# Attention and two expert layers on one core: token rows of the first block turned later, routing lists in two tables, probabilities stored as 18 rows, the second block's list loaded ahead of its weights

## The chip, the cores and the metric

The kernel runs on one core of a Trainium2 chip. The metric is device microseconds (us) of one execution. Before the change three runs gave 1200.1 (median), 1199.29 and 1203.38 us.

## What is computed

```python
def reference(**kwargs):
    attn_out = _attn_ref(**attn_kwargs)          # q halved by mean of pairs, softmax(q k^T / 8) v
    x = attn_out.transpose(0, 2, 1, 3).reshape(B, S, H * D)     # 4 x 576 tokens of 512
    x = _moe_ref(x=x, **moe_kwargs)              # r * ((relu(xk w_k))**2 w_v), r = sigmoid(xr w_r)
    return _moe2_ref(x=x, **moe2_kwargs)

def _moe2_ref(x, w_gate, w_local, w1, w2):       # 8 experts, one for each token
    logits = x @ w_gate
    local_gate = sigmoid(x @ w_local)
    # along a row of tokens: e = argmax(logits) where s == 0 or local_gate < 0.5, else the token before's e
    out[b, s] = softmax(logits)[e] * (relu(x[b, s] @ w1[e]) @ w2[e])
```

There are 32 heads of 1152 keys and 576 pooled queries, 2304 tokens, and eight experts of 512 x 1024 and 1024 x 512. Products of float32 are made as three matmuls of a high and a low part.

## The kernel before, in words

The program is one stream, written out by hand in a fixed order; every engine works its own part of it in that order. Names: PE is TensorE, ACT ScalarE, DVE VectorE, POOL GpSimd, and SP is the engine that issues most DMAs. An engine that waits holds up everything behind it on that engine.

**Attention** (to about 540 us) is not touched.

**The first layer** works on units `u` of 256 tokens (two tiles `i` of 128), 0 to 8. For a unit, `hidden` makes one of four groups of 256 hidden features (24 matmuls of 128x256), `square` squares them on ACT and makes the low part on POOL (L748), `gate` makes the sigmoid gate of a tile (12 matmuls), `value` the second product (24 matmuls), and `product` (L774) multiplies and stores the rows to `x2d` in DRAM. `logits` (L783) makes nine dot products on DVE for a tile, each over two operands in SBUF. `mix` and `mix_split` prepare the next units' inputs; the low part is made on POOL (L568). In the loop over `u` (2 to 7) the parts of neighbouring units are interleaved.

**Routing** runs behind it, a unit at a time: `route1` (DVE) makes `kg`, `route2` turns it into a row on PE (L832), ACT copies it (L836), a DVE scan carries the expert along the tokens (`erow`, L838), `route3` spreads it over the partitions (L849, `oh` at L850), and `route4` counts the places (L857 to L869) and scatters the token numbers into the table `tbl` in DRAM: two indirect DMAs on POOL, one for each tile (L871). Both write the same tile, so the second waits until the first has landed.

**The second layer** works on blocks of up to 512 tokens of one expert. `early` (in unit 7) picks the largest expert from units 0 to 6, loads the block's list of tokens (`load_ids(0)`, L1015), its first weights (`load_w`), and gathers its rows (`gather_x(0, 0)`, L1029). The last unit, 8, is written out after the loop; in it `transpose_x(0)` turns the gathered rows on PE (L1054) and `gather_x(0, 2)` fetches the other half, right after the first `gate`. Weights come as raw chunks (0.5 MB each, L988 and L994) that `split_w` cuts into a high part on ACT (L1010) and a low part on DVE (L1011). `up` is the first product of a block (L1068), `down` the second (L1085), `finish` scales the rows by their probability (`pgs`) on ACT and scatters them to the output (L1093, L1094). A block with at most 128 tokens in a pair of tiles runs `lone_up` and `lone_down` (L1120, L1140).

After block 0's first half, the list of all blocks is made (`block_list`, `block_list2`), SP reads it into registers (`block_regs`, L977 and L978), loads five chunks of block 1's weights, then the lists of blocks 1 and 2, and stores the probabilities: `probabilities` ends with one DMA from 128 partitions x 18 to the 2304 places of `pd` (L1217), 4 bytes each. `gather_x(1, 0)` and `gather_p` (L1037, the probabilities of block 0's tokens) follow on POOL. All engines read the block counts into registers (L1355, L1356). Then `NH0[0] = 2` chunks of block 1 are split before block 0's second half goes through `up`; then come `finish` of the first half, `next_x(0)` (the rows of block 1 are turned, those of block 2 gathered), the other splits, and the second half's `down`. From there `block(j)` repeats for j = 1 to 12, the later ones only as far as the list has blocks.

Of the kernel before, what the change touches and what calls it, by code (L numbers as in the profile page):

```python
# [37 lines left out]
def kernel(  # L38
# [39 lines left out]
    tbl = dram.tile([E * NTS, 1], I32, name="tbl")  # L78
# [41 lines left out]
    ids = [cp.tile([P, 4], I32, name=f"ids{i}") for i in range(4)]  # L120
    pgs = [cp.tile([P, 4], F32, name=f"pg{i}") for i in range(2)]
# [11 lines left out]
    def constants2(tp, ci, pi):  # L133
# [3 lines left out]
        nc.gpsimd.iota(tid, pattern=[[P, NT]], base=0, channel_multiplier=1)  # L137
# [21 lines left out]
    def constants3(tp):  # L159
# [5 lines left out]
        nc.sync.dma_start(tbl.rearrange("(p f) o -> p (f o)", p=P), pad)  # L165
# [688 lines left out]
    def route4(u):  # L854
# [15 lines left out]
        for i in range(2):  # L870
            nc.gpsimd.indirect_dma_start(  # L871
                out=tbl, out_offset=bass.IndirectOffsetOnAxis(ap=si[:, i : i + 1], axis=0),
                in_=tid[:, 2 * u + i : 2 * u + i + 1], in_offset=None,
            )
# [96 lines left out]
    NH0 = (2, 2, 0)  # L971
# [41 lines left out]
    def load_ids(j):  # L1013
        if j <= JX:
            nc.sync.dma_start(  # L1015
                ids[j % 4], tbl[bass.ds(regs[j][1], 512), :].rearrange("(i p) o -> p (i o)", p=P),
                allow_slow_non_contiguous=True,
            )


    def gather_x(j, t):
        if j > JX:
            return
        for i in range(2):
            ix = bass.IndirectOffsetOnAxis(ap=ids[j % 4][:, t + i : t + i + 1], axis=0)
            if j:
                nc.gpsimd.indirect_dma_start(out=XGB[j % 2][:, i], out_offset=None, in_=x2d, in_offset=ix)
            else:
                nc.gpsimd.indirect_dma_start(  # L1029
                    out=XGB[0][:, i], out_offset=None, in_=x2d[0 : 256 * (NU - 2)], in_offset=ix,  # L1030
                    bounds_check=256 * (NU - 2) - 1, oob_is_err=False,
                )
# [170 lines left out]
    def probabilities():  # L1203
# [13 lines left out]
        nc.sync.dma_start(  # L1217
            pd[0:NTOK].rearrange("(t p) o -> p (t o)", p=P), pe, allow_slow_non_contiguous=True
        )
# [70 lines left out]
    transpose_x(0)  # L1290
    gather_x(0, 2)
# [6 lines left out]
    product(u, 0, py[1])  # L1298
    split_w(1)
# [43 lines left out]
    for j in (1, 2):  # L1343
        block_regs(j, lst[:, 0, j - 1 : j], lst[:, 1, j - 1 : j])
    for s in range(8, 8 + NRAW):
        load_w(s)
    load_ids(1)
    load_ids(2)
    probabilities()
    gather_x(1, 0)  # L1350
    gather_p(0, 0)
    gather_p(0, 2)
    down(0, 2)
    down(0, 3)
# [106 lines left out]
```

## Time and profile before

| what | value |
|---|---|
| median of three runs | 1200.1 us |
| the profiled execution's own time, its span | 1199.74 us, 1198.0 us |
| PE busy | 1080.2 us, 90% |
| DVE, ACT, POOL busy | 828.2, 718.6, 575.3 us |
| DMA | 156.31 MB, 130 GB/s in the mean |
| POOL's wait at L871 for the scatter before it | 67.2 us in 9 waits |

The profile is one execution. Times in its rows are microseconds from the span's start; an engine's row in the timeline gives start, duration, engine, line, operation, tiles and shapes, and in square brackets the idle time before it with what ended it. A `q` behind an engine's name is its sequencer: register reads, branches and the issue of DMAs. PE is busy nearly all the time from the attention's end on, so the places where it stands idle are the ones to look for; there are few, and three groups of them lie where the change works: in the steps of the loop over `u` (640 to 830 us), in unit 8 (830 to 858 us) and around the start of the second block (888 to 916 us).

### The profile page before, as it was taken

How to read it: one execution, taken by the hardware profiler on the slowest of the kernel's cores; microseconds unless marked ns; L12 is line 12 of the kernel's file. 1: busy time of each engine (PE TensorE's matmuls, PEld its weight loads, DVE VectorE, ACT ScalarE, POOL GpSimd, SP SyncE). 2: the span in 40 equal slices, each digit the busy share in tenths (PEclk: the TensorE clock that was granted, in tenths of full speed). 3: DMA queues.
4: the chain of work that ended last, by engine and by line, in shares of the span. 5: the costliest groups of instructions: out<-in, count | busy, mean ns of one | idle time of the engine just before them, and what ended most of it. 6: DMA issues, size and time to landing. Idle time of an engine off the chain costs nothing. (4 is left out here: it accounts for less than half of the span.)

```text
span 1198.0 us, 18084 instructions
## 1 busy us (share of the span) xinstructions
PE 1080.2 (90%) x6073; PEld 910.6 (76%) x6073; DVE 828.2 (69%) x1255; ACT 718.6 (60%) x1006; POOL 575.3 (48%) x392
## 2 busy tenths in 40 slices
PE   7899999999999999978999989897987999998875
PEld 6677777777777777767887878776776888876764
DVE  6888888888888888889955665685353544446544
ACT  5787777777777777767775444341333535446543
POOL 2556666666666666468734333342213514144233
PEclk9999999999999999998999999998897999999988
DMA  9166666656566564515520322203646756556765
GB/s 198 32 132 148 138 142 141 140 130 131 131 149 141 137 138 100 157 45 172 182 98 10 36 31 32 36 18 89 117 81 153 253 178 202 176 179 213 251 205 176
DMA packets 147348, 156.31 MB, mean 130 GB/s; under 512 B 62993, under 2 KB 115857, under 8 KB 146324
## 3 DMA queue, kind: packets, MB, share of 16 engines
q1 hardware_dynamic: 140836, 141.51, 47.4%
q0 software_dynamic: 6384, 13.15, 3.7%
q8 instruction: 73, 1.20, 0.5%
q14 instruction: 55, 0.45, 0.1%
HBM read 107.30 MB, written 15.58 MB: 103 GB/s over the span
## 5 line engine op out<-in xcount | busy, mean ns | idle before, releaser
L403 PE MATMUL pvt<-sr,V 128*128 128x288 f32 x1152 | 328.5, 409 | 31.4 <-ACT xc L416 14.7
L403 PEld LDWEIGHTS pvt<-sr,V 128*128 128x128 f32 x1152 | 202.1, 190 | 71.2 <-POOL sr L389 17.9
L345 PE MATMUL pt<-kw 128*128 128x288 f32 x1152 | 247.3, 337 | 5.5 <-DVE Mt L357 4.1
L389 POOL TENSOR_TENSOR sr<-sr,Mb 128x576 f32<-128x576 f32 x96 | 142.5, 1487 | 195.3 <-ACT Mb L380 159.5
L357 DVE TENSOR_TENSOR Mt<-Mt,pt 128x576 f32<-128x576 f32 x224 | 168.1, 750 | 76.2 <-ACT sr L349 74.3
L349 ACT ACTIVATE sr<-pt 128x576 f32<-128x576 f32 x288 | 181.5, 646 | 54.6 <-PE pt L345 52.4
L345 PEld LDWEIGHTS pt<-kw 128*128 128x128 f32 x1152 | 177.6, 189 | 34.8 <-DVE Mt L357 10.4
L396 ACT ACTIVATE sr<-sr 128x1728 f32<-128x1728 f32 x96 | 157.9, 1644 | 52.0 <-DVE sr L390 46.4
L390 DVE TENSOR_TENSOR sr<-sr,Mb 128x1152 f32<-128x1152 f32 x96 | 160.9, 1676 | 2.8 <-ACT Mb L380 2.8
L727 PE MATMUL ph<-a,wk 128*128 128x256 f32 x864 | 108.4, 286 | 0.9 <-ACT kr L745 0.4
L727 PEld LDWEIGHTS ph<-a,wk 128*128 128x128 f32 x864 | 106.5, 193 | 2.6 <-ACT kr L745 1.0
L767 PE MATMUL py<-kw,sq 128*128 128x512 f32 x312 | 84.3, 423 | 0.0
L1068 PE MATMUL ph<-a,wk 128*128 128x256 f32 x576 | 73.4, 288 | 6.3 <-PEq L1415 5.8
L1085 PE MATMUL py<-kw,sq 128*128 128x512 f32 x324 | 78.3, 398 | 0.0
L1068 PEld LDWEIGHTS ph<-a,wk 128*128 128x128 f32 x576 | 71.3, 195 | 8.8 <-issue 7.7
L871 POOL DMA_INDIRECT tbl<-tid,si x18 | 18.4, 1021 | 122.9 <-DMA tbl<-tid,si 67.2
L745 ACT ACTIVATE kr<-ph 128x512 f32<-128x512 f32 x36 | 21.3, 592 | 92.4 <-PE ph L727 57.2
L446 POOL TENSOR_TENSOR xo<-xc,t 64x576 f32<-64x576 f32 x32 | 73.1, 2283 | 1.2
L783 DVE CUSTOM_DVE_ANT_0 a<-r,wg 128x512 f32<-128x512 f32 x96 | 71.4, 744 | 3.1
L767 PEld LDWEIGHTS py<-kw,sq 128*128 128x128 f32 x312 | 62.1, 203 | 15.0 <-issue 0.2
L1085 PEld LDWEIGHTS py<-kw,sq 128*128 128x128 f32 x324 | 60.8, 189 | 14.5
L1037 POOL DMA_INDIRECT pg<-pd,ids x44 | 44.4, 1009 | 37.4 <-DMA pg<-pd,ids 15.7
(250 smaller groups left out, 1756.7 us busy)
## 6 DMA issues: line engine op xcount, KB each, us to landing
wraw<-in_moe_w_dram SPq DMA_DIRECT2D x101, 512.0 KB
kw<-Hk SPq DMA_DIRECT2D x224, 72.0 KB
ql<-in_q_dram SPq DMA_DIRECT2D x16, 576.0 KB
kl<-in_k_dram SPq DMA_DIRECT2D x64, 144.0 KB
V<-in_v_dram SPq DMA_DIRECT2D x128, 72.0 KB
kw<-Hq SPq DMA_DIRECT2D x112, 72.0 KB
kw<-kw SPq DMA_DIRECT2D x14, 576.0 KB
xTd<-xo SPq DMA_DIRECT2D x16, 288.0 KB
```

Source lines behind the costliest of these rows:

```text
L345: nc.tensor.matmul(pt[:, i, :HT], lhsT=lhs, rhs=qh[:, hl, hd, i, :], start=(hl == 0), stop=(hl == 1))
L349: nc.scalar.activation(out=Sg[h, kt], in_=ptt[h, kt][:, :, :HT], func=AF.Copy)
L357: nc.vector.tensor_tensor(out=Mt[h], in0=a, in1=pt[:, :, :HT], op=ALU.max)
L389: nc.gpsimd.tensor_tensor(out=s[:, 0], in0=s[:, 0], in1=Mb[h], op=ALU.subtract)
L390: nc.vector.tensor_tensor(out=s[:, 1:3], in0=s[:, 1:3], in1=Mb[h].unsqueeze(1).to_broadcast([P, 2, T]), op=ALU.subtract)
L396: nc.scalar.activation(out=s, in_=s, func=AF.Exp, scale=scale)
L403: nc.tensor.matmul(pvt[h][:, i, :HT], lhsT=V[(h // 2) % 2][:, kt, c : c + P], rhs=Sg[h, kt][:, i], start=(kt == 0), stop=(kt == KT - 1),)
L446: nc.gpsimd.tensor_tensor(out=xo[p].rearrange("p (i t c) -> p i c t", i=2, c=9)[a], in0=y[a], in1=t2[a], op=ALU.mult)
L727: nc.tensor.matmul(pt[:, i], lhsT=wk[:, wl, g, c, P * i : P * i + P], rhs=a[:, xl, c], start=(n == 0), stop=(n == 11))
L767: nc.tensor.matmul(p_v, lhsT=SQ[u, f // 2][:, xl, f % 2, s], rhs=wv[:, wl, f], start=(f == 0 and n == 0), stop=(f == 7 and n == 2),)
L1068: nc.tensor.matmul(pt[:, i], lhsT=w[:, wl, g, c, P * i : P * i + P], rhs=x[:, xl, c], start=(n == 0), stop=(n == 11))
L1085: nc.tensor.matmul(py[i], lhsT=hs[:, xl, f, P * i : P * i + P], rhs=w[:, wl, 2 * g + f], start=(g == 0 and n == 0), stop=(g == 3 and n == 5),)
```

## The change

The table `tbl` becomes two, `tbl[0]` for even tiles and `tbl[1]` for odd ones. The first is filled with 2304 as before, the second with 0; the numbers written to the second are smaller by 2304, so that the sum of both lists is the token number. `load_ids` loads two lists, and `gather_x` adds them on POOL. The rows of block 0 are turned, and its other half gathered, behind unit 8's first `value` and `product`. The second block's list is loaded ahead of its weights. The first two splits of block 1 (`NH0[0]`: 2 becomes 0) stand behind block 0's `up` and `finish`. The probabilities are turned on PE into 18 rows of 128 and stored as rows; their store and `gather_p` stand behind block 0's last two `down` groups.

```diff
@@ -75,7 +75,7 @@
     xTd = dram.tile([DM, NTOK], F32, name="xTd")
     x2d = dram.tile([NTOK + 1, DM], F32, name="x2d")
     pd = dram.tile([NTOK + 1, 1], F32, name="pd")
-    tbl = dram.tile([E * NTS, 1], I32, name="tbl")
+    tbl = [dram.tile([E * NTS, 1], I32, name=f"tbl{i}") for i in range(2)]
 
     ctx.enter_context(tc.manual_schedule())
 
@@ -118,6 +118,7 @@
     nks = cp.tile([1, 8], I32, name="nks")
     wgt = cp.tile([P, 4, E + 1], F32, name="wgt")
     ids = [cp.tile([P, 4], I32, name=f"ids{i}") for i in range(4)]
+    idb = [cp.tile([P, 4], I32, name=f"idb{i}") for i in range(2)]
     pgs = [cp.tile([P, 4], F32, name=f"pg{i}") for i in range(2)]
 
     io = dict(allow_small_or_imprecise_dtypes=True)
@@ -134,7 +135,9 @@
         nc.gpsimd.iota(im8, pattern=[[1, E]], base=-E, channel_multiplier=0, **io)
         nc.gpsimd.iota(base, pattern=[[NTS, E]], base=0, channel_multiplier=0, **io)
         nc.gpsimd.iota(base0, pattern=[[NTS, E]], base=0, channel_multiplier=0, **io)
-        nc.gpsimd.iota(tid, pattern=[[P, NT]], base=0, channel_multiplier=1)
+        nc.gpsimd.iota(
+            tid.rearrange("p (u i) -> p u i", i=2), pattern=[[2 * P, NU], [P - NTOK, 2]], base=0, channel_multiplier=1
+        )
         nc.gpsimd.iota(k128, pattern=[[-P, 4 * NK]], base=0, channel_multiplier=0, **io)
         nc.gpsimd.iota(i4, pattern=[[1, 4]], base=1, channel_multiplier=0, **io)
         nc.gpsimd.iota(cc, pattern=[[1, NC]], base=0, channel_multiplier=0, **io)
@@ -162,7 +165,10 @@
         nc.vector.tensor_scalar(out=om, in0=mus, scalar1=-1.0, scalar2=1.0, op0=ALU.mult, op1=ALU.add)
         pad = tp.tile([P, E * NTS // P], I32, name="pad")
         nc.gpsimd.memset(pad, NTOK)
-        nc.sync.dma_start(tbl.rearrange("(p f) o -> p (f o)", p=P), pad)
+        nc.sync.dma_start(tbl[0].rearrange("(p f) o -> p (f o)", p=P), pad)
+        pad0 = tp.tile([P, E * NTS // P], I32, name="pad0")
+        nc.gpsimd.memset(pad0, 0)
+        nc.sync.dma_start(tbl[1].rearrange("(p f) o -> p (f o)", p=P), pad0)
         z = tp.tile([1, DM], F32, name="z")
         nc.gpsimd.memset(z, 0.0)
         nc.sync.dma_start(x2d[NTOK : NTOK + 1, :], z)
@@ -869,7 +875,7 @@
         nc.vector.tensor_tensor(out=base, in0=base, in1=p3[:, 2], op=ALU.add)
         for i in range(2):
             nc.gpsimd.indirect_dma_start(
-                out=tbl, out_offset=bass.IndirectOffsetOnAxis(ap=si[:, i : i + 1], axis=0),
+                out=tbl[i], out_offset=bass.IndirectOffsetOnAxis(ap=si[:, i : i + 1], axis=0),
                 in_=tid[:, 2 * u + i : 2 * u + i + 1], in_offset=None,
             )
 
@@ -968,7 +974,7 @@
     XGB = [xg0, None]
     NRAW = 5
     regs = {}
-    NH0 = (2, 2, 0)
+    NH0 = (0, 2, 0)
     NH1 = (2, 4, 2)
     NH2 = (8, 8, 6)
 
@@ -1012,15 +1018,18 @@
 
     def load_ids(j):
         if j <= JX:
-            nc.sync.dma_start(
-                ids[j % 4], tbl[bass.ds(regs[j][1], 512), :].rearrange("(i p) o -> p (i o)", p=P),
-                allow_slow_non_contiguous=True,
-            )
+            for t, to in zip(tbl, (ids[j % 4], idb[j % 2])):
+                nc.sync.dma_start(
+                    to, t[bass.ds(regs[j][1], 512), :].rearrange("(i p) o -> p (i o)", p=P),
+                    allow_slow_non_contiguous=True,
+                )
 
 
     def gather_x(j, t):
         if j > JX:
             return
+        if t == 0:
+            nc.gpsimd.tensor_tensor(out=ids[j % 4], in0=ids[j % 4], in1=idb[j % 2], op=ALU.add)
         for i in range(2):
             ix = bass.IndirectOffsetOnAxis(ap=ids[j % 4][:, t + i : t + i + 1], axis=0)
             if j:
@@ -1214,9 +1223,14 @@
         pe = rp.tile([P, NT], F32, name="pe")
         nc.vector.tensor_reduce(out=pe, in_=ls, axis=AX.X, op=ALU.add)
         nc.vector.tensor_tensor(out=pe, in0=pe, in1=sm, op=ALU.mult)
-        nc.sync.dma_start(
-            pd[0:NTOK].rearrange("(t p) o -> p (t o)", p=P), pe, allow_slow_non_contiguous=True
-        )
+        return pe, ls
+
+
+    def store_p(pe, ls):
+        nc.tensor.transpose(p23[0:NT, 0:P], pe, ident)
+        row = ls.rearrange("p t e -> p (t e)")[0:NT, 0:P]
+        nc.vector.tensor_copy(row, p23[0:NT, 0:P])
+        nc.sync.dma_start(pd[0:NTOK].rearrange("(t p) o -> t (p o)", p=P), row)
 
 
     def first_block():
@@ -1287,8 +1301,6 @@
 
     u = NU - 1
     gate(u, 0, py[0])
-    transpose_x(0)
-    gather_x(0, 2)
     route2(u - 1)
     split_w(0)
     load_w(3)
@@ -1296,6 +1308,8 @@
     route3(u - 1)
     value(u, 0, py[1], range(4, 8))
     product(u, 0, py[1])
+    transpose_x(0)
+    gather_x(0, 2)
     split_w(1)
     load_w(4)
     gate(u, 1, py[0])
@@ -1342,16 +1356,17 @@
     ys = [a32, wloc]
     for j in (1, 2):
         block_regs(j, lst[:, 0, j - 1 : j], lst[:, 1, j - 1 : j])
+    load_ids(1)
     for s in range(8, 8 + NRAW):
         load_w(s)
-    load_ids(1)
     load_ids(2)
-    probabilities()
+    pe, ls = probabilities()
     gather_x(1, 0)
+    down(0, 2)
+    down(0, 3)
+    store_p(pe, ls)
     gather_p(0, 0)
     gather_p(0, 2)
-    down(0, 2)
-    down(0, 3)
     n0 = nc.values_load(lst0[:, 2:3], min_val=0, max_val=512)
     nk = [nc.values_load(nks[:, i : i + 1], min_val=0, max_val=JX) if i != 4 else None for i in range(8)]
     for j in range(3, JX + 1):
```

On **PE**, in unit 8: from the first `gate` (L758, L764 in the change) to the second. Before (`ptx` holds the turned rows, `xg` the gathered ones, `kg` and `erow` are routing's):

```order
L758 MATMUL py_4751<-wr,a_4899 128x512 x12
L1054 MATMUL ptx_4884<-ident,xg_4333 128x128 x4
L1054 MATMUL ptx_4885<-ident,xg_4333 128x128 x4
L832 LDWEIGHTS kg
L832 MATMUL p_4753<-identb,kg 1x128
...
L767 MATMUL py_4752<-kw,sq_4887 128x512 x6
L767 MATMUL py_4752<-kw,sq_4888 128x512 x6
L849 MATMUL p_4754<-onesb,erow 128x8
...
L767 MATMUL py_4752<-kw,sq_4894 128x512 x6
L767 MATMUL py_4752<-kw,sq_4895 128x512 x6
L758 MATMUL py_4751<-wr,a_4899 128x512 x12
```

and now:

```order
L764 MATMUL py_4757<-wr,a_4905 128x512 x12
L838 LDWEIGHTS kg
L838 MATMUL p_4759<-identb,kg 1x128
...
L773 MATMUL py_4758<-kw,sq_4893 128x512 x6
L773 MATMUL py_4758<-kw,sq_4894 128x512 x6
L855 MATMUL p_4760<-onesb,erow 128x8
...
L773 MATMUL py_4758<-kw,sq_4900 128x512 x6
L773 MATMUL py_4758<-kw,sq_4901 128x512 x6
L1063 MATMUL ptx_4890<-ident,xg_4339 128x128 x4
L1063 MATMUL ptx_4891<-ident,xg_4339 128x128 x4
L764 MATMUL py_4757<-wr,a_4905 128x512 x12
```

The eight transposes went from ahead of the 24 `value` matmuls to behind them.

On **SP**, from the reading of the second and third block's numbers (`lst`) to the store of the probabilities (`wraw` are weights, `ids` and `idb` lists). Before:

```order
L977 TENSOR_LOAD lst
L978 TENSOR_LOAD lst
L988 DMA wraw_7663<-in_moe_w_dram 128x4x256
L988 DMA wraw_7664<-in_moe_w_dram 128x4x256
...
L994 DMA wraw_4332<-in_moe_w_dram 128x2x512
L1015 DMA ids_98<-tbl 128x4x1
L1015 DMA ids_99<-tbl 128x4x1
L1217 DMA pd<-pe 128x18x1
```

and now:

```order
L983 TENSOR_LOAD lst
L984 TENSOR_LOAD lst
L1022 DMA ids_99<-tbl_60 128x4x1
L1022 DMA idb_103<-tbl_61 128x4x1
L994 DMA wraw_7671<-in_moe_w_dram 128x4x256
L994 DMA wraw_7672<-in_moe_w_dram 128x4x256
...
L1000 DMA wraw_4338<-in_moe_w_dram 128x2x512
L1022 DMA ids_100<-tbl_60 128x4x1
L1022 DMA idb_102<-tbl_61 128x4x1
L1233 DMA pd<-ls 18x128
```

The second block's list, as two loads, went ahead of the five chunks; the third block's lists and the store kept their place behind them.

On **ACT**, from the register reads to the first turned rows of block 1 (`w1b` are block 1's weights, `kw` and `sq` block 0's hidden features, `a` and `wloc` its results). Before:

```order
L1356 TENSOR_LOAD nks x7
L1010 ACTIVATE w1b<-wraw_7663 128x1024
L1010 ACTIVATE w1b<-wraw_7664 128x1024
L1074 ACTIVATE kw<-p_4753 128x512
...
L1093 ACTIVATE a_4334<-py_4751,pg_101 128x512
L1093 ACTIVATE wloc<-py_4752,pg_101 128x512
L1057 ACTIVATE a_4326<-ptx_4884 128x512
```

and now:

```order
L1371 TENSOR_LOAD nks x7
L1083 ACTIVATE kw<-p_4759 128x512
...
L1102 ACTIVATE a_4340<-py_4757,pg_104 128x512
L1102 ACTIVATE wloc<-py_4758,pg_104 128x512
L1016 ACTIVATE w1b<-wraw_7671 128x1024
L1016 ACTIVATE w1b<-wraw_7672 128x1024
L1066 ACTIVATE a_4332<-ptx_4890 128x512
```

The two splits went from ahead of block 0's second half to behind the results of its first half. On POOL, each pair of scatters now names two tables where it named one.

## Rows read from the trace of the kernel before

**Rows 1.** Costliest groups: line, engine, operation, tiles, count, then busy us and mean ns.

```profile
L783 DVE CUSTOM_DVE_ANT_0 a<-r,wg 128x512 f32<-128x512 f32 x96 | 71.4, 744 | 3.1
```

**Rows 2.** Timeline of PE, the steps of units 2 to 7.

```profile
652.21 0.17 PE L857 MATMUL p<-oh,trib 128*128 128x8 bf16 x1 [2.98 <-DVE oh L850]
659.56 11.68 PE L727 MATMUL ph<-a,wk 128*128 128x256 f32 x96
689.29 11.67 PE L727 MATMUL ph<-a,wk 128*128 128x256 f32 x96
805.09 0.47 PE L832 MATMUL p<-identb,kg 128*1 128x128 bf16 x4 [1.90 <-DVE kg L822]
821.54 5.91 PE L727 MATMUL ph<-a,wk 128*128 128x256 f32 x48
```

**Rows 3.** Timeline of POOL and then DVE in two of these steps.

```profile
669.23 0.96 POOL L871 DMA_INDIRECT tbl<-tid,si  x1 [8.59 <-DMA tbl<-tid,si]
797.73 2.41 POOL L568 TENSOR_TENSOR a<-m,a 128x1024 fp32r<-128x1024 f32 x1
800.08 1.28 POOL L748 TENSOR_TENSOR kw<-kr,kw 128x512 fp32r<-128x512 f32 x1
801.33 1.29 POOL L748 TENSOR_TENSOR sq<-kr,sq 128x512 fp32r<-128x512 f32 x1
797.64 5.53 DVE L783 CUSTOM_DVE_ANT_0 a<-r,wloc 128x512 f32<-128x512 f32 x1
```

**Rows 4.** Timeline of PE in unit 8.

```profile
837.23 0.45 PE L1054 MATMUL ptx<-ident,xg 128*128 128x128 f32 x1 [7.00 <-DMA xg<-x2d,ids]
845.10 3.07 PE L767 MATMUL py<-kw,sq 128*128 128x512 f32 x12
848.00 2.91 PE L758 MATMUL py<-wr,a 128*128 128x512 f32 x12
```

**Rows 5.** Timeline of POOL and of SP's queue ahead of unit 8.

```profile
819.50 1.38 POOL L871 DMA_INDIRECT tbl<-tid,si  x1 [6.24 <-DMA tbl<-tid,si]
829.49 1.03 POOL L1029 DMA_INDIRECT xg<-x2d,ids  x1 [8.61 <-issue]
831.85 2.48 POOL L748 TENSOR_TENSOR sq<-kr,sq 128x512 fp32r<-128x512 f32 x2
825.19 0.41 SPq L1015 DMA_DIRECT2D ids<-tbl  x1
```

**Rows 6.** Timeline of PE around the second block's start.

```profile
888.00 5.91 PE L1068 MATMUL p<-a,wk 128*128 128x256 f32 x48
899.44 8.73 PE L1068 MATMUL p<-a,wk 128*128 128x256 f32 x48 [5.53 <-DVE kw L1075]
912.87 0.45 PE L1054 MATMUL ptx<-ident,xg 128*128 128x128 f32 x1 [4.70 <-DMA xg<-x2d,ids]
915.53 2.93 PE L1085 MATMUL py<-kw 128*128 128x512 f32 x6
```

**Rows 7.** Timeline of DVE, SP's queue and POOL in the same stretch.

```profile
885.79 0.18 DVE L1216 TENSOR_TENSOR pe<-pe,sm 128x18 f32<-128x18 f32 x1
886.35 2.21 SPq L988 DMA_DIRECT2D wraw<-in_moe_w_dram  x4
896.27 0.93 SPq L1015 DMA_DIRECT2D ids<-tbl  x2
897.25 0.50 SPq L1217 DMA_DIRECT2D pd<-pe  x1
886.50 0.97 POOL L871 DMA_INDIRECT tbl<-tid,si  x1 [8.29 <-DMA tbl<-tid,si]
901.72 0.98 POOL L1027 DMA_INDIRECT xg<-x2d,ids  x1 [14.24 <-DMA ids<-tbl]
912.06 0.94 POOL L1037 DMA_INDIRECT pg<-pd,ids  x1 [8.10 <-DMA pd<-pe]
```

**Rows 8.** L1356, register reads on PE's queue: ns min/median/max, first and last start.

```profile
L1356 PEldq TENSOR_LOAD <-nks x7: 300/307/315, 884.4 to 886.9; - x7
```

## The prediction

> **What bounds the kernel now.** I read the page first: PE is the busiest engine by far, so the question is where PE stands idle and what ends each idle time. For that I went through the timeline of PE from the attention's end on, and at each gap through the timelines of the engine that ended it. Three places belong to this change. In the routing steps PE waits for DVE at tiny matmuls [rows 2], because POOL sits still for 8.59 us between the two scatters of a pair [rows 3] and its elementwise work, on which ACT and then DVE depend, comes late. In unit 8 PE waits 7.00 us for the gathered rows [rows 4]. At the second block PE waits 5.53 us for block 0's low parts and 4.70 us for block 1's rows, and runs slowly behind both [rows 6]. The sum below is made against the profiled execution's own 1199.74 us; the median of the runs is 0.4 higher.
>
> **A. Two tables, in the routing steps.** What the steps lose now: PE starts the same 96 matmuls at 659.56 and again at 689.29 [rows 2]; this step of 29.7 us is nearly free of waits. From 659.56 to 821.54 there are five steps, 162.0 us, so 162.0 - 5 x 29.7 = 13.3 us go to waits and to slow matmuls behind them, 2.7 a step. The wait of 2.98 at 652.21 lies ahead of them. All of it back is 16.3 us, the upper bound.
>
> With two tables the second scatter can issue right behind the first (about 1.3 us, 0.96 and an issue gap), and POOL's work of that step starts some 8 us earlier. It is one L568 and four L748: 2.41 + 4 x 1.29 = 7.6 us [rows 3]. That brings it under the nine dot products of DVE, and there it has a price: a dot has a mean of 0.74 us [rows 1], and the one at 797.64, begun 0.09 us ahead of three POOL operations, lasted 5.53, to 0.5 us past their end [rows 3]. PE then stood 1.90 us for `kg` [rows 2]. That is the one step of the five whose scatter happened to land early, so it is a look at the changed order. For a quiet step: the dots of the second tile take 9 x 0.74 = 6.7 us and end, with the product ahead of them and the routing operations behind, some 8.5 us after the step's start (estimate); PE asks for `kg` after the 96 matmuls, 11.7 us, and a gate of 2.9 [rows 2, 4], at 14.6. With 5 us of POOL's work on top `kg` comes at 13.5, in time; with all 7.6 at 16.1, and PE waits 1.5 and runs slowly afterwards, about 3.3 us a step. I take 2.0 a step, between 0 and 3.3, because the last L748 depends on PE's last hidden group and falls partly behind the dots. So 5 x (2.7 - 2.0) = 3.5, and 2.5 of the 2.98: **gain 6.0**, bounds -3.0 (5 x 2.7 - 5 x 3.3) and 16.3.
>
> [...]
>
> **B. Rows turned later, in unit 8.** The wait of 7.00 ends at 837.23, so the first gate was over at 830.2; the second begins at 848.0 [rows 4]. Between them lie 17.8 us. The work in it at full speed is 24 `value` matmuls, 2 x 3.07 less some overlap, 5.9, eight transposes (1.0, estimate) and the routing row (0.6): 7.5. The rest, 10.3, is the upper bound. PE now does the routing row and `value` first and reaches the transposes at 837.0 without a wait. Are the rows there? Today the second scatter issues at 819.50, 6.24 us after the first was done; SP starts the list 5.7 us later, POOL gathers 4.3 us after that, and the rows land 7.7 us after the gather's start [rows 4, 5]. Now both scatters are out by 814.5 and landed by about 820; two list loads and the add on POOL (no such row; above 0, below the 1.29 of an operation on 128 times as much [rows 3]; I take 0.2, since it is so small) bring the gather to 825, the rows to 833. So the transposes find them. But the two L748 that stand at 831.85 behind the gather (2.48 us) [rows 5] move up under DVE's last dots and routing operations, by the price of A; if all of it delays `kg`, PE waits 2.5 at the routing row and loses 1.6 more to slow matmuls. I take half: 10.3 - 2.0 = **8.3**, bounds 6 and 10.3. The other half's gather moves behind the transposes with them; it is needed only when block 0's second half is turned, after four groups of `up`.
>
> **C. Around the second block.** Today: second scatter 886.50, list 896.27, gather 901.72, rows 912.87; probabilities stored at 897.25, landed at 912.06 [rows 6, 7]. The change, in order:
> - The second scatter issues at about 878.5 (the first went at 877.2: 886.50 less 8.29 and 0.97) and lands 8 to 9.8 us later, so SP takes the list at about 887.5. The weights start some 2 us later than 886.35; nothing waits for them on PE before the second block's `lone_up`.
> - The list lands in the 5.4 us of today, 892.9; with add and issue the gather goes at 893.4, 8.3 us earlier. Rows land 7.7 (as in B) to 11.2 us (as today) later: 901.1 to 904.6.
> - PE's register reads ran ahead of the matmuls, from about 884 to 887.2 [rows 8]. Now they stand behind a transpose that waits for `pe`, ready at 885.97 [rows 7]. So `up` begins some 2.3 us after 888.0. What is queued behind is PE's alone. **Cost 2.3**, inside the next lines.
> - The splits no longer stand ahead of ACT's work on `up`; the wait of 5.53 goes, and the 48 matmuls behind it take 5.9 instead of 8.73 [rows 6]. `up` ends at 890.3 + 11.8 = 902.1, where it ended at 908.2. The splits come later, where DVE and ACT wait for the probabilities anyway.
> - The store of the probabilities goes after the five chunks, at about 893. Its 2304 places of 4 bytes took 14.8 us; as 18 rows it is bounded from below by the 4.3 us of the quickest list (825.19 to 829.49 [rows 5]) and from above by 14.8. The nearest row is the list of 896.27, also behind these weights, 5.4 us; I add what the weights, 2 us later than today, hold it up: landed at 902.
> - From there the gather of probabilities, ACT's scaling and PE's restart take 3.5 us (912.06 to 915.53). PE restarts at 905.5: **gain 10**, less 0.5 for a rest of 1 us on the turned rows: 9.5. Bounds: store landed at 907.7, 911.2, gain 4.3; and PE bound, 902.1 and 1.1 for the transposes, 12.3.
>
> What follows is PE's own work in large part, so the gain passes on.
>
> **D. What is added.** 13 more list loads on SP (0.4 us each [rows 5]), an add on POOL in each block, one more fill of a table during the attention. In the block loop the list is loaded a block ahead and SP, POOL and the rows have slack; cover gone, an add of 1.29 in each of ten blocks would be 13. I take **0.8**, bounds 0 and 2.
>
> **Sum**: 6.0 + 8.3 + 9.5 - 0.8 = 23.0; 1199.74 - 23.0 = 1176.7, against the median **1177**.
>
> **Rivals.**
> 1. *The dots keep POOL out* (or POOL's work slips between them): A gives all 16.3 and B 10.3, so 16.3 + 10.3 + 9.5 - 0.8 = 35.3, **1164**. [...] Against: the dot of 797.64. Chance 0.20.
> 2. *POOL's work blocks DVE in full* and takes the place of the waits for the scatters: A -3.0, B 6: 11.7, **1188**. For it: 5.53 us [rows 3]. Against: the last L748 comes late. Chance 0.15.
> 3. *The second scatter still waits*, for the queue and not for the table: then A gives nothing, the lists come no earlier, B keeps some 8 and C perhaps 2: **1190**. Against: gathers of one pair, into one tile, issue one behind the other (both lie between 829.49 and 831.85 [rows 5]). Chance 0.06.
> 4. *Slower: the second list delays the weights.* The 2304 single places took 14.8 us, 6.4 ns each, so 512 more in each of some eleven blocks are 3.3 us, 36 in all, if they hold up chunks for which PE waits; it decides from 2.1 us a block (23.0 / 11). The time would be 1199.7 - 23.0 + 36 = **1213**. Against: PE runs the blocks with few waits, the chunks are loaded five ahead. Chance 0.04.
>
> **Numbers.** The forecast has a chance of 0.55, with a range of its own of 1170 to 1185. The likely cases are all on one side. The range that holds 8 in 10 runs from 1163 (rival 1 with its spread) to 1190 (rivals 2 and 3); the bounds of the sum, 38.9 and 5.3 us, would be 1161 and 1195. A difference of 0.3%, 3.6 us, is about what a measurement of this kernel can tell from none: faster 0.93 (forecast, rivals 1 and 2, most of 3), same 0.03, slower 0.04.
>
> **What would show it.** A: POOL's scatters in pairs 1.3 us apart, no wait for a scatter; PE's step near 31.7 us, dots of 2 us and more on DVE, and PE's waits at the routing row (`kg`) in place of `oh` and `erow`. A step of 29.7 says rival 1, 33 rival 2. B: transposes behind `value` with a wait under 1 us, 7.5 to 12 us between the two gates. C: the list some 9 us ahead of today, no wait of `up` for `kw`, a start of `up` 2 us late, PE back at `down` about 16 us after the first `up` matmul of block 0's second half instead of 27.5. D: the block loop as long as today. A block loop longer by over 10 us, or scatters still 8 us apart, would make the prediction wrong.

## The result, and the profile after

The changed kernel takes **1171.24 us** (median of 4 runs, 1169.12 to 1173.31); the kernel before took 1199.69 (4 runs, 1199.13 to 1203.38). The ratio is 0.9756, 95% interval 0.9730 to 0.9783: 2.4% faster. The profiled execution, the slowest of the four, has a span of 1171.1 us against 1198.0, so 26.9 us are to be found in the traces.

They are found in stages, from one row of PE to the next: the first `gate` of unit 2; the last `hidden` pair of unit 7; the two `gate`s of unit 8; the restart of `down` in block 0's second half; block 2's `up`. Each row of the view gives the stage, its length, then the busy time (and the number of instructions) of PE, of its weight loads, of DVE, ACT and POOL, then PE's granted clock as a share of full speed (**PEclk**), the DMA share and GB/s. Kernel before:

```profile
637.13:659.56 22.43, 19.45 (x85) 14.96 (x84) 16.83 (x36) 9.32 (x17) 6.07 (x5) 0.92 0.04 12
659.56:821.54 161.98, 151.67 (x896) 129.51 (x895) 109.66 (x301) 65.05 (x115) 59.95 (x42) 0.97 0.21 28
827.29:848.00 20.71, 13.43 (x52) 9.91 (x51) 5.99 (x17) 6.06 (x9) 6.98 (x6) 0.75 0.58 178
848.00:915.53 67.53, 54.60 (x338) 48.66 (x336) 26.68 (x64) 17.89 (x25) 13.48 (x11) 0.90 0.57 87
915.53:942.98 27.45, 26.47 (x113) 20.89 (x113) 17.55 (x18) 18.61 (x24) 11.88 (x11) 0.93 0.86 281
942.98:1183.85 240.87, 222.47 (x1320) 192.72 (x1320) 122.64 (x131) 117.13 (x155) 88.21 (x79) 0.99 0.63 198
```

The same stages of the changed kernel:

```profile
638.69:656.65 17.96, 17.90 (x85) 13.78 (x84) 12.58 (x30) 9.21 (x17) 6.03 (x5) 1.00 0.05 15
656.65:806.61 149.96, 146.86 (x897) 126.08 (x896) 130.02 (x308) 66.33 (x115) 64.52 (x42) 1.00 0.21 31
812.35:824.50 12.15, 10.15 (x53) 7.63 (x51) 7.58 (x16) 4.15 (x7) 3.06 (x3) 1.00 0.54 192
824.50:882.50 58.00, 49.60 (x340) 43.77 (x338) 25.49 (x65) 17.99 (x26) 15.85 (x14) 0.99 0.56 110
882.50:915.75 33.25, 28.65 (x113) 22.70 (x113) 22.17 (x22) 21.67 (x27) 13.52 (x13) 0.87 0.75 239
915.75:1156.09 240.34, 224.68 (x1320) 194.13 (x1320) 120.55 (x129) 116.01 (x154) 90.87 (x89) 0.98 0.63 197
```

Routing steps (the first two lines): 184.4 became 167.9, **16.5 less**. Unit 8: **8.6 less**. Second gate to the restart: **9.5 less**. Restart to block 2: **5.8 more**. The blocks after it: 0.5 less. The start (638.69 against 637.13) and the end take 1.6 and 0.9 more, and 0.01 falls between the lines: 16.5 + 8.6 + 9.5 - 5.8 + 0.5 - 1.6 - 0.9 = 26.8, with rounding. The 1.6 at the start is no cost of the change that these traces show: unit 2's first `gate` lies between 635.4 and 638.8 us in the fourteen profiles of this document, in no order of the edits.

What answers to [rows 1]: DVE's dots became longer, 744 to 976 ns in the mean.

```profile
L789 DVE CUSTOM_DVE_ANT_0 a<-r,wg 128x512 f32<-128x512 f32 x96 | 93.7, 976 | 3.1
```

In the routing steps, what answers to [rows 2, 3]; timeline of POOL, then DVE, then PE, in the step that begins at 687.59 (start, duration; idle time before in brackets). PE's first two rows are of the step before, one of the two that wait:

```profile
687.74 0.99 POOL L877 DMA_INDIRECT tbl<-tid,si  x1 [7.42 <-DVE base L875]
689.03 1.06 POOL L877 DMA_INDIRECT tbl<-tid,si  x1 [0.30 <-issue]
690.11 2.41 POOL L574 TENSOR_TENSOR a<-m,a 128x1024 fp32r<-128x1024 f32 x1
...
695.65 1.76 POOL L754 TENSOR_TENSOR sq<-kr,sq 128x512 fp32r<-128x512 f32 x1 [1.41 <-ACT kr L753]
690.04 3.04 DVE L789 CUSTOM_DVE_ANT_0 a<-r,wg 128x512 f32<-128x512 f32 x1
...
695.57 0.69 DVE L789 CUSTOM_DVE_ANT_0 a<-r,wg 128x512 f32<-128x512 f32 x1
...
701.22 0.16 DVE L831 SCALAR_TENSOR_TENSOR kg<-kg,f 128x2 bf16<-128x2 bf16 x1
672.60 0.47 PE L838 MATMUL p<-identb,kg 128*1 128x128 bf16 x4 [1.52 <-DVE kg L828]
673.00 1.66 PE L773 MATMUL py<-kw 128*128 128x512 f32 x6
...
701.94 0.38 PE L838 MATMUL p<-identb,kg 128*1 128x128 bf16 x4
```

The scatters are 1.3 us apart, and none waits for the one before it. The dots are stretched as foreseen, but `kg` is there at 701.38 and PE asks for it at 701.94. Only two of the five steps wait, 1.5 us each, with fast matmuls behind. The steps take 30.9, 29.4, 31.0, 29.3 and 29.3 us.

Around the second block, what answers to [rows 4 to 7]; timeline of PE, of SP's queue and POOL, and of ACT, all of the changed kernel:

```profile
817.27 0.47 PE L838 MATMUL p<-identb,kg 128*1 128x128 bf16 x4 [2.00 <-DVE kg L828]
864.85 11.78 PE L1077 MATMUL p<-a,wk 128*128 128x256 f32 x96 [1.52 <-issue]
882.50 2.93 PE L1094 MATMUL py<-kw 128*128 128x512 f32 x6 [3.81 <-ACT a L1102]
904.40 1.74 PE L1138 MATMUL p<-ident,kr 128*128 128x128 f32 x8 [2.53 <-ACT kr L1133]
915.75 11.77 PE L1077 MATMUL ph<-a,wk 128*128 128x256 f32 x96 [1.92 <-PEq L1430]
...
861.53 0.38 SPq L1022 DMA_DIRECT2D ids<-tbl  x1
870.43 2.57 SPq L1233 DMA_DIRECT2D pd<-ls  x1
890.37 1.85 SPq L1000 DMA_DIRECT2D wraw<-in_moe_w_dram  x3
868.69 0.99 POOL L1036 DMA_INDIRECT xg<-x2d,ids  x1 [0.63 <-POOL ids L1032]
879.07 0.94 POOL L1046 DMA_INDIRECT pg<-pd,ids  x1 [8.13 <-DMA pd<-ls]
...
894.12 1.06 ACT L1016 ACTIVATE w2b<-wraw 128x1024 fp32r<-128x1024 f32 x1 [4.69 <-DMA wraw<-in_moe_w_dram]
896.28 1.06 ACT L1016 ACTIVATE w2b<-wraw 128x1024 fp32r<-128x1024 f32 x1 [1.10 <-DMA wraw<-in_moe_w_dram]
899.75 1.06 ACT L1016 ACTIVATE w2b<-wraw 128x1024 fp32r<-128x1024 f32 x1 [2.40 <-DMA wraw<-in_moe_w_dram]
```

The list, the rows and the store come about as worked out, the list 2.5 us earlier. New is the end: between the store (issued to 873.0) and 890.37 SP makes 28 register reads, and the three weight chunks behind these reads come late. The first of the reads, and the group that holds the last of them (three of its thirteen are earlier ones):

```profile
L1370 SPq TENSOR_LOAD <-lst x1: 510/510/510, 873.0 to 873.0; - x1
L984 SPq TENSOR_LOAD <-lst x13: 262/264/277, 799.5 to 889.2; - x13
```

ACT waits 4.69, 1.10 and 2.40 us for the chunks, its scaling and `kr` stand behind, and PE waits for `kr`. Before, the same chunks went out when PE restarted, at 915.53 [rows 6]:

```profile
915.50 4.76 SPq L994 DMA_DIRECT2D wraw<-in_moe_w_dram  x3
```

Now they go 7.9 us after the restart.

### The profile page after: what moved, and what is told of

Its sections match the earlier page's. It is cut to its first block, busy times and chain, and to the rows that moved or that the text cites. A ratio compares the mean times of both kernels' runs of the same rounds, so it can differ in the third digit from the quotient of the medians.

```text
span 1171.1 us, 18157 instructions
## 1 busy us (share of the span) xinstructions
PE 1072.9 (92%) x6074; PEld 905.2 (77%) x6074; DVE 847.8 (72%) x1256; ACT 719.8 (61%) x1006; POOL 585.2 (50%) x406
## 5 line engine op out<-in xcount | busy, mean ns | idle before, releaser
L409 PE MATMUL pvt<-sr,V 128*128 128x288 f32 x1152 | 330.8, 412 | 28.7 <-ACT xc L422 14.4
L363 DVE TENSOR_TENSOR Mt<-Mt,pt 128x576 f32<-128x576 f32 x224 | 167.9, 749 | 77.0 <-ACT sr L355 75.2
L789 DVE CUSTOM_DVE_ANT_0 a<-r,wg 128x512 f32<-128x512 f32 x96 | 93.7, 976 | 3.1
L1094 PE MATMUL py<-kw,sq 128*128 128x512 f32 x324 | 78.9, 401 | 0.0
L773 PE MATMUL py<-kw,sq 128*128 128x512 f32 x312 | 77.9, 399 | 0.0
L1077 PEld LDWEIGHTS ph<-a,wk 128*128 128x128 f32 x576 | 69.7, 191 | 8.1 <-issue 7.0
L1094 PEld LDWEIGHTS py<-kw,sq 128*128 128x128 f32 x324 | 61.4, 191 | 14.5
L773 PEld LDWEIGHTS py<-kw,sq 128*128 128x128 f32 x312 | 57.5, 188 | 13.5
L574 POOL TENSOR_TENSOR a<-m,a 128x1024 fp32r<-128x1024 f32 x18 | 44.1, 2453 | 42.3 <-ACT a L573 37.4
```

What stands on the lines that cost most here:

```text
L363: nc.vector.tensor_tensor(out=Mt[h], in0=a, in1=pt[:, :, :HT], op=ALU.max)
L409: nc.tensor.matmul(pvt[h][:, i, :HT], lhsT=V[(h // 2) % 2][:, kt, c : c + P], rhs=Sg[h, kt][:, i], start=(kt == 0), stop=(kt == KT - 1),)
L773: nc.tensor.matmul(p_v, lhsT=SQ[u, f // 2][:, xl, f % 2, s], rhs=wv[:, wl, f], start=(f == 0 and n == 0), stop=(f == 7 and n == 2),)
L789: nc.vector.tensor_tensor_reduce(out=a32, in0=x2, in1=wg[:, e] if e < E else wloc, scale=1.0, scalar=0.0, op0=ALU.mult, op1=ALU.add, accum ...
L1077: nc.tensor.matmul(pt[:, i], lhsT=w[:, wl, g, c, P * i : P * i + P], rhs=x[:, xl, c], start=(n == 0), stop=(n == 11))
L1094: nc.tensor.matmul(py[i], lhsT=hs[:, xl, f, P * i : P * i + P], rhs=w[:, wl, 2 * g + f], start=(g == 0 and n == 0), stop=(g == 3 and n == 5),)
```

## The experiments

All times of stages come from PE's timeline, as above: **R** routing steps, **G** gate to gate in unit 8, **S** second gate to restart, **T** restart to block 2's `up`. The ratio is to the kernel before, run beside it.

| kernel | R | G | S | T | ratio (95% interval) |
|---|---|---|---|---|---|
| before | 184.4 | 20.7 | 67.5 | 27.5 | 1 |
| changed | 167.9 | 12.2 | 58.0 | 33.3 | 0.9756 (0.9730 to 0.9783) |
| e1 tables alone | 168.3 | 12.1 | 68.8 | 27.0 | 0.9828 (0.9805 to 0.9851) |
| e2 rows later alone | 185.1 | 11.1 | 69.7 | 27.6 | 0.9925 (0.9896 to 0.9955) |
| e3 second block alone | 186.9 | 19.4 | 61.1 | 28.6 | 0.9975 (0.9938 to 1.0013) |
| e4 single places | 168.3 | 13.7 | 69.4 | 27.5 | 0.9824 (0.9806 to 0.9842) |
| e5 reads moved | 167.9 | 13.7 | 60.7 | 28.6 | 0.9717 (0.9684 to 0.9750) |
| e6 and block 2's lists | 168.3 | 13.9 | 55.8 | 27.2 | 0.9715 (0.9682 to 0.9747) |
| e7 more on POOL | 183.3 | 13.8 | 58.7 | 35.1 | 0.9899 (0.9855 to 0.9943) |
| e8 POOL's mix somewhat later | 167.3 | 13.7 | 58.7 | 33.7 | 0.9772 (0.9739 to 0.9805) |
| e9 rows early | 167.9 | 15.3 | 57.7 | 33.8 | 0.9796 (0.9764 to 0.9827) |
| e10 e6, `kg` covered | 169.5 | 10.8 | 57.1 | 28.5 | 0.9701 (0.9664 to 0.9738) |
| e11 changed, again | 167.9 | 12.2 | 57.5 | 35.0 | 0.9768 (0.9729 to 0.9806) |
| e12 e10 in unit 8 alone | 167.9 | 11.0 | 57.8 | 28.3 | 0.9699 (0.9646 to 0.9752) |

### One part at a time: e1, e2, e3

Each is the kernel before with the hunks of one part of the diff: e1 `tbl`, `idb`, `tid` and the add; e2 the two lines below; e3 the order around the second block, `store_p` and `NH0`.

```diff
     gate(u, 0, py[0])
-    transpose_x(0)
-    gather_x(0, 2)
...
     product(u, 0, py[1])
+    transpose_x(0)
+    gather_x(0, 2)
```

> The kernel before with the two tables alone (two list loads, the add). Theory 'slack': the dots of DVE are stretched by POOL's earlier work, but the 6 us by which kg came ahead of PE's need take nearly all of it; the first gate of unit 2 to the hidden pair of unit 7 gets some 16 us shorter, and the lists come some 8 us earlier besides, which spares part of unit 8's wait for the gathered rows (up to 7) and moves the second block's list by nothing much, since it still stands behind the weights: 1174 to 1184. Theory 'price', as predicted: 2.0 us a step stay lost, the routing steps gain 6 alone: 1190 to 1195. Theory 'the gain needs the rows turned later': about 1195.

> The kernel before with the first block's rows turned, and its other half gathered, behind the first value of unit 8, and nothing else; one table. Theory of the sum: the wait of 7.0 us for the gathered rows goes and the gain is about 8, 1192, whether or not there are two tables, since the rows landed at 837.2 and PE comes to the transposes at about 837. Rival: with one table the rows are just late, or kg is (POOL's low parts in front of the gather): PE waits 2 to 5 us at another place, 1195 to 1198.

> The kernel before with the parts around the second block alone: list of block 1 ahead of its weights, splits behind the first layer of block 0's second half, probabilities as 18 rows; one table. Theory: these earn 9.5 us up to the restart of the second layer, less what the scatter's wait of 8.3 us costs the list (it still starts late, at about 895), and some 5.8 us are given back in block 1, where the raw weights behind SP's register reads come too late for ACT's splits: net 2 to 5, 1195 to 1198. Rival: the give-back belongs to something else in the whole change (the earlier start of everything, the second table's lists) and does not show here: 1190.

Medians: 1177.60, 1193.66 and 1195.75 us, beside 1201.61 of the kernel before: e1 and e3 are within the range of their first expectation, e2 is nearest to it. By the ratios e1 saves 20.6 us of 1200, e2 9.0 and e3 3.0, which its interval does not tell from nothing. Among these three and the changed kernel, R is short where there are two tables and long where there is one: the 16 us belong to the tables. G is short in e1 and in e2: 12.1 without turning the rows later, 11.1 without the tables. Either edit removes most of the wait of 7.00 us [rows 4], e1 because the list and the rows come earlier, e2 because PE asks later. So the parts should add up to more than the whole; they do by their middles (20.6 + 9.0 + 3.0 = 32.6 against 1199.7 x 0.0244 = 29.3), but the intervals of 2.8, 3.5 and 4.5 us either way are too wide to show it.

e3's time was in the expected range, but not for the expected reasons alone. S got 6.4 us shorter; T gave back 1.1 and not 5.8, and R was 2.5 longer in this execution. On T it is the rival that was right: the loss belongs to something in the whole change. What that is comes out with e5.

### The store as 2304 places again: e4

```diff
-        nc.tensor.transpose(p23[0:NT, 0:P], pe, ident)
-        row = ls.rearrange("p t e -> p (t e)")[0:NT, 0:P]
-        nc.vector.tensor_copy(row, p23[0:NT, 0:P])
-        nc.sync.dma_start(pd[0:NTOK].rearrange("(t p) o -> t (p o)", p=P), row)
+        nc.sync.dma_start(
+            pd[0:NTOK].rearrange("(t p) o -> p (t o)", p=P), pe, allow_slow_non_contiguous=True
+        )
```

> The changed kernel with the probabilities stored as 2304 single places again, at the same place in SP's order and without the transpose on PE. Theory: the store lands some 5 to 9 us later than as 18 rows (14.8 against 8.1 us or less), PE's restart waits for it by as much, and part comes back because the raw weights, late anyway, then hide part: slower than the changed kernel by 3 to 8, 1174 to 1179. Rival: the weights' late chunks set the end of block 1's first part whatever the store does: within 2 us of the changed kernel.

Timeline of POOL, then PE, then SP's queue, in e4:

```profile
890.37 0.94 POOL L1046 DMA_INDIRECT pg<-pd,ids  x1 [17.83 <-DMA pd<-pe]
881.46 0.45 PE L1063 MATMUL ptx<-ident,xg 128*128 128x128 f32 x1 [5.58 <-DMA xg<-x2d,ids]
893.84 2.93 PE L1094 MATMUL py<-kw 128*128 128x512 f32 x6 [8.77 <-ACT a L1102]
871.96 2.84 SPq L1230 DMA_DIRECT2D pd<-pe  x1
```

The store, issued at 871.96, is waited for until 890.4, 18.4 us; the 18 rows took from 870.43 to 879.1, 8.6. The gathered rows suffer too: PE waits 5.58 us for them, in the changed kernel not at all. S is 11.4 longer, T 5.7 shorter; by the ratios e4 is 0.0068, 8 us, slower (1178.31 us), the upper end of what was expected. Two things follow. Without the rows nothing is left of S's gain (67.5 before, 69.4 here); what the earlier list and the later splits give by themselves was not tried. And T is not a fixed loss: here PE restarts later, and the three weight chunks go out only 3.4 us behind the restart, at 897.28.

### The reads on SP: e5 and e6

e5 moves 20 of the 28 reads, those for blocks 3 and on; below it, what e6 adds:

```diff
-    for j in range(3, JX + 1):
-        block_regs(j, lst[:, 0, j - 1 : j], lst[:, 1, j - 1 : j])
...
     def block(j):
+        if j + 2 <= JX:
+            block_regs(j + 2, lst[:, 0, j + 1 : j + 2], lst[:, 1, j + 1 : j + 2])
         load_ids(j + 2)
```

```diff
-    load_ids(2)
     pe, ls = probabilities()
...
     store_p(pe, ls)
+    load_ids(2)
     gather_p(0, 0)
```

> The changed kernel with SP's reads of the list entries of blocks 3 and on moved: each pair is read at the start of the block two ahead of it, not all in one row behind the store of the probabilities. Theory: the three chunks that SP issued at 890.37 then go as soon as the split of chunk 8 has freed its buffer, at about 886, ACT's waits for raw weights (4.69, 1.10 and 2.40 us) shrink by some 4.5, and the part from PE's restart to block 2 takes 28 to 29 us instead of 33.25: 4 to 5 faster than the changed kernel, 1166 to 1168. Rival: the buffers or the DMA queues set the time of these chunks, not the reads: within 1.5 us of the changed kernel. Other rival: the two reads at each block's start (1.8 us) make a later block's weights late: slower than the changed kernel.

> The kernel of e5_regs, and besides the lists of block 2 loaded behind the store of the probabilities instead of ahead of it. Theory: SP issues the store 2.4 us earlier (the lists' two loads took 868.01 to 870.3), it lands earlier by about that, and PE's wait of 3.81 us at the restart falls to about 1.5: another 2 us faster than e5_regs, 1164 to 1166. Rival: the store lands when the five chunks ahead of it have landed, whatever SP does: as e5_regs, within 1.

Timeline of SP's queue, then PE, in e5:

```profile
889.73 3.84 SPq L1000 DMA_DIRECT2D wraw<-in_moe_w_dram  x3
886.21 2.93 PE L1094 MATMUL py<-kw 128*128 128x512 f32 x6 [3.94 <-ACT a L1102]
914.82 11.77 PE L1077 MATMUL ph<-a,wk 128*128 128x256 f32 x96 [0.75 <-PEq L1430]
```

T fell from 33.3 to 28.6 in e5, as expected: 4.7 of the 5.8 us came back. By the ratio e5 is 0.0039 (beside the first runs of the changed kernel) or 0.0051 (beside e11) better, 5 to 6 us, with intervals that overlap, so it is the stage that shows it, and not the medians. Its own profile shows less over the whole, since S was 2.7 longer in it (a wait of 2.20 us for `xg`, and slow matmuls, 24 of them in 4.33 us from 845.40, in the changed kernel 3.14 from 844.28). The chunks now wait for their buffer: SP sat 7.3 us for the split on DVE and issued 3.5 us after the restart.

The other traces agree. In nine of the fourteen kernels the three chunks go out between 2.1 us ahead of PE's restart (e1, e2) and 6.2 us behind it (e3), and T is 27.0 to 28.6. In the other five (the changed kernel, e7, e8, e9, e11) they go out 7.9 to 9.8 us behind it, and T is 33.3 to 35.1. e1 and e3 are among the nine, so each part by itself loses little; only with both does PE restart that far ahead of the end of the reads.

In e6, whose lines follow, the store goes out 42.6 us after the second gate instead of 45.9 and PE waits 1.69 us at the restart instead of 3.81:

```profile
866.97 1.11 SPq L1233 DMA_DIRECT2D pd<-ls  x1
883.77 3.84 SPq L1000 DMA_DIRECT2D wraw<-in_moe_w_dram  x3
880.18 2.42 PE L1094 MATMUL py<-kw 128*128 128x512 f32 x6 [1.69 <-ACT a L1102]
```

Beside e5, on the same chip, its median is 2.1 us lower (1165.95 to 1168.09), as expected, but the two ratios and intervals are nearly the same, as the rival had it: e6's own part is seen in the trace and not in the runs.

### POOL against the dots: e7 and e8

e7 makes POOL's low part of the second mix twice. e8 moves it in the program behind the four groups of the hidden layer; since the squares of the last two come later, POOL makes it behind two of the four low parts of the squares, and not behind all four as its expectation says.

```diff
             mix_split(u + 2, 1)
+            m, a = MB[1], AB[1][u % 2]
+            nc.gpsimd.tensor_tensor(out=a[:, 1], in0=m, in1=a[:, 0], op=ALU.subtract)
```

```diff
-            mix_split(u + 2, 1)
+            m, a = MB[1], AB[1][u % 2]
+            nc.scalar.activation(out=a[:, 0], in_=m, func=AF.Copy)
...
         hidden(u + 1, 3)
+        if u + 2 < NU:
+            nc.gpsimd.tensor_tensor(out=a[:, 1], in0=m, in1=a[:, 0], op=ALU.subtract)
         route1(u)
```

> The changed kernel with POOL's low part of the second mix made twice in each of the five steps of the loop (a second operation of 2.41 us into the same place with the same values, right behind the first). Theory 'slack': the stretch of the dots has used up the 6 us by which kg came early, so further work of POOL under the dots goes straight to PE: waits of some 2 us at the routing row in each step, and where such a wait is followed by slow matmuls another 1.5: 8 to 16 us slower than the changed kernel, 1179 to 1187. Rival: POOL's work slips between the dots without holding them up: within 2 us of the changed kernel.

> The changed kernel with POOL's low part of the second mix (2.41 us) moved from right behind the scatters to behind the four low parts of the squares, so that it meets none of DVE's dot products. Theory 'slack': the dots of a step are stretched by some 2.5 us less, kg comes 2 us earlier, and PE's two waits of 1.5 us at the routing row go (the other three steps had none): 3 us faster than the changed kernel, about 1168, and the dots of 3 to 4.3 us become 0.7 to 2. Rival: POOL's squares then start at once behind the scatters and stretch the dots by as much: no change, within 1 us. A step of 29.3 us each is the best case.

Timeline of PE in e7, the first two of five such waits, and of DVE in e8, the first step:

```profile
673.71 0.47 PE L838 MATMUL p<-identb,kg 128*1 128x128 bf16 x4 [3.36 <-DVE kg L828]
706.96 0.47 PE L838 MATMUL p<-identb,kg 128*1 128x128 bf16 x4 [2.31 <-DVE kg L828]
```

```profile
664.54 2.79 DVE L789 CUSTOM_DVE_ANT_0 a<-r,wloc 128x512 f32<-128x512 f32 x1
...
667.45 1.07 DVE L823 TENSOR_TENSOR eq<-L,mx 128x16 f32<-128x16 f32 x1
668.55 1.20 DVE L824 TENSOR_TENSOR eq<-eq,im 128x16 f32<-128x16 f32 x1
```

In e7 five operations of 2.41 us cost R 15.4 us: the waits are 13.7 us in sum instead of 3.05, and matmuls run slowly behind some (24 took 7.26 us behind the wait of 3.38 at 739.76, and 5.87 at 641.12 without a wait). The median of 1190.9 is above the expected range; it is 15.7 us above e11, the changed kernel on the same chip, where 8 to 16 were expected. The change had used up the slack of `kg` (the time by which it is there before PE asks for it), and a further 2.41 us of POOL's work under the dots is not free any more. In e8 the waits only fell from 1.52 to 1.06; the moved operation still met the last dot, and the squares behind it the small routing operations (1.07 and 1.20 us, of some 0.17). The ratio shows no gain, as the rival says. An order in which this operation meets no dot was not tried.

### The rows turned early, with two tables: e9

It takes e2's two lines back out of the changed kernel.

> The changed kernel with the first block's rows turned, and its other half gathered, where they stood before, right behind unit 8's first gate; everything else as changed. Theory from e1_tables: with two tables the rows have landed about when PE comes to them (a wait of 1.4 us there, and a gate-to-gate time of 12.1 as in the changed kernel), so turning them later earns nothing more: within 1.5 us of the changed kernel, 1170 to 1173. Rival, by the predicted sum: turning them later earns about 8 by itself: 1177 to 1180.

PE waited 2.64 and 0.64 us for the rows, and G was 15.3. The ratio lies 0.0028 to 0.0040 above that of the changed kernel (3.4 to 4.8 us), with intervals that overlap. Neither expectation was met; with two tables, turning the rows later is worth between nothing (e1's G) and some 3 to 5 us (e9's G and ratio), not 8.

### Covering `kg`, and the changed kernel again: e10, e11, e12

e10 does this on top of e6 (in unit 8 the other `value` parts follow, so that no matmul is made twice); e12 leaves the first hunk, the loop's, out.

```diff
         gate(u, 0, py[0])
+        if u + 2 < NU:
+            value(u, 0, py[1], range(2))
         route2(u - 1)
...
-            value(u, 0, py[1])
+            value(u, 0, py[1], range(2, 8))
...
     gate(u, 0, py[0])
+    value(u, 0, py[1], range(2))
     route2(u - 1)
...
-    up(0, 1, 1)
     route1(u)
+    up(0, 1, 1)
     route2(u)
```

> The kernel of e6_regs_l2, and besides PE does six matmuls of the value product ahead of the routing row in the loop and in unit 8 (so that kg's lateness of 1.5 to 2.2 us is covered by work), and the DVE operations that make the last unit's kg stand ahead of PE's last half of up(0, 1) and so ahead of that group's low part on DVE. Theory: the waits of 1.52 (two steps), 2.00 to 2.25 and 2.25 at the routing rows go, and the slow matmuls behind the last two (about 1.5 each): 7 to 10 us faster than e6_regs_l2, 1156 to 1159. Rival: the routing chain gets later by the six matmuls, so that erow or oh is waited for instead: within 2 us of e6_regs_l2.

> The changed kernel itself once more, beside the kernels of this call on the same chip: 1169 to 1174, and a second look at whether the wait of 2.00 us for kg in unit 8 is followed by slow matmuls (gate to gate 13.7 us, as in e4, e5 and e8) or not (12.15, as in its first profile).

> The kernel of e6_regs_l2 with e10's two edits in unit 8 alone (six matmuls of the value product ahead of the routing row; the last unit's kg ahead of PE's last half of up(0, 1)), and the loop as it was. Theory: the loop's 1.2 us that e10 lost go back to 168.3 from 169.5, the two gates of unit 8 lie about 10.8 us apart and the second gate to the second half's up takes 38.9: a ratio to the kernel before of 0.967 to 0.970, 2 us better than e10. Rival: the scatters, lists and the store of the probabilities bound PE's restart, so what unit 8 gains is waited for there: as e6, 0.971 to 0.972.

Unit 8 gained what was expected, G 10.8 and 11.0. The loop lost 1.2 in e10, where `oh` is waited for instead (1.30 and 1.27 us) and `kg` in the last step (1.35). And what unit 8 gained was waited for at the restart, S being 57.1 and 57.8 instead of e6's 55.8: from unit 2's first gate to block 2 e6 takes 270.9, e10 271.6, e12 270.7. So the rivals hold, for e10 in the time too (1167.52 us); e12's ratio lies in the range of its first expectation, but its interval takes in the rival's as well. e11, the changed kernel again, came out at 1175.25 us, above its range of 1169 to 1174, and its wait of 2.04 us in unit 8 was once more followed by fast matmuls (G 12.2). e6, e10 and e12 are the best kernels tried, 0.970 to 0.9715 of the time before, some 5 to 8 us below the changed kernel, and not to be told apart.

## Why the prediction came out as it did

The forecast was 1177 and its own range 1170 to 1185; 1171.24 lies near its lower end. Two terms came out at their size, one was far too small, and one loss was missing. That the time fell into the range is in part luck: A's 10.5 us more would by themselves have made it 1166.5, below the range, and the 5.8 us lost behind the restart brought it back.

- **A, the tables: 16.5, not 6.0.** The mechanism was right: the scatters go as pairs, POOL's work falls under the dots, and the dots are stretched (3.04 us instead of 0.69). The mis-sized term was "I take 2.0 a step, between 0 and 3.3". The same paragraph had the sum that decides: with 5 us of POOL's work on top, `kg` comes at 13.5 and PE asks at 14.6. Measured: 13.8 against 14.4 in the step at 687.59. Three steps paid nothing, two 1.5 and no slow matmuls behind: 0.6 a step. 1.4 x 5 = 7.0 of the error is this; the step without waits is 29.4 us and not 29.7, another 1.6; and the time ahead of 659.56 gave 4.5 instead of 2.5, since the 24 `value` matmuls behind the wait of 2.98 had been slow too (7.39 us, now 5.83). These last two are also why 16.5 is above the prediction's upper bound of 16.3. By its own signs (a step of 31.7 us, of 29.7 for rival 1) the mean step of 30.0 speaks for rival 1: that rival's amount for A came true, by slack and not by dots that keep POOL out; rival 2 had the right collision and the wrong price. e7 shows how near that was: one more operation of 2.41 us in each step, and the gain of R is gone.
- **B, the rows: 8.6 measured, 8.3 predicted.** The size was right and the wait on `kg` too (2.00 us; 2.5 was the estimate). But by G either edit alone gains as much (e1 8.6, e2 9.6), and beside the tables the turning is worth 0 to 5 us (e1, e9). The prediction put the whole down to the turning. A sum over parts cannot show that; each part was priced with the others in place.
- **C, the second block: 9.5 and 9.5.** In us from the second gate, first as predicted and then as measured: the list was taken at 39.5 and 37.0, the gather went at 45.4 and 44.2, `up` began at 42.3 and 40.4, the store was issued at 45 and 45.9 and had landed at 54 and 54.6, and PE restarted at 57.5 (58.0 with the half us taken off for the turned rows) and 58.0. `up` began 2 us earlier than predicted: PE stood 1.52 us in front of it and not 2.3, and 24 matmuls on the way took 3.14 us, in the kernel before 4.64. That changed nothing, for the store, and not `up`, set the restart.
- **What failed: "What follows is PE's own work in large part, so the gain passes on."** 5.8 of the 9.5 were given back at once. SP's reads were as long before (897.8 to 915.5; in the changed kernel 873.0 to 890.4), but ended with PE's restart and were hidden; now PE restarts 7.9 us ahead of the chunks behind them. e5, without most of the reads, gets 4.7 of the 5.8 back, so they were the cause. The prediction had priced PE's reads [rows 8] and put SP's at nothing.
- **D** cost nothing that the trace shows: the blocks took 240.3 instead of 240.9. Rivals 3 and 4 are out: no scatter waits for another, and the block loop is no longer with the second list.

The sum with what was measured: 16.5 + 8.6 + 9.5 - 5.8 + 0.5 = 29.3, less 2.5 at the start and end.

## What to carry to other kernels

Where two engines begin to collide, don't price the collision by its length: work out by how much the last result of the slowed engine is early, charge what goes beyond, and note how much is left. When a chain is shortened, look up what was issued beside it, above all behind a row of register reads (28 took SP 17.4 us here), and when it will now land against when it will be asked for. Parts that remove the same wait are to be priced alone as well as together.

## What was not expected of the hardware

The same wait of PE is followed by slow matmuls in some executions and not in others. In the changed kernel and in e5 PE does twelve gate matmuls in 2.92 us, waits 2.00 us for `kg`, and goes on with the same twelve matmuls. In the changed kernel they take 3.07 us at a granted clock of 1.00 (e11 3.06 us); in e5 4.63 us, with a mean granted clock of 0.59 in the stretch (e4 4.60 us, e8 4.62). The twelve matmuls and the stretch that begins with the wait's end, of the changed kernel and then of e5:

```profile
817.67 3.07 PE L773 MATMUL py<-kw,sq 128*128 128x512 f32 x12
817.27:820.70 3.43, 3.43 (x17) 2.38 (x18) 2.10 (x3) 1.53 (x2) 0.00 (x0) 1.00 0.09 36
```

```profile
817.10 4.63 PE L773 MATMUL py<-kw,sq 128*128 128x512 f32 x12
816.71:820.70 3.99, 3.99 (x13) 3.07 (x14) 2.10 (x3) 1.53 (x2) 0.00 (x0) 0.59 0.18 69
```

So the price of such a wait was 2.0 or 3.6 us, and nothing in the rows ahead of it told which.

And the collision of DVE and POOL goes both ways: POOL's operation of 1.28 us (701.41) took 1.76 under the dots (695.65). A dot had begun 0.08 us ahead of it (695.57) and kept its usual 0.69 us. But the dot of 690.04 also began 0.07 us ahead of POOL's operation, that of 690.11, and lasted 3.04 us, until 0.56 us past that one's end. Spans on POOL are rough, so the order of two starts that near is not settled.
